# Linear attention and a token and channel mixer on one core: the first batch's intermediates are laid into buffers of later weights, and U and V are converted one pair later

## The chip, the core and the metric

The kernel runs on one core of a Trainium2 chip. The metric is the device time of one execution in microseconds (us), the median of three runs. All inputs are in DRAM at the start and the output is in DRAM at the end. A profiled execution of the kernel before is the source of the rows below.

## What is computed

```python
def phi(x):
    proj = np.einsum('bhsd,df->bhsf', x, w_phi)
    proj = proj - np.max(np.abs(proj), axis=-1, keepdims=True)
    return np.concatenate([np.exp(proj), np.exp(-proj)], axis=-1)
q_p, k_p = phi(q), phi(k)                       # q, k, v: (8, 8, 576, 64), w_phi: (64, 128)
kv = np.einsum('bhsf,bhsd->bhfd', k_p, v)
z = np.sum(k_p, axis=2)
num = np.einsum('bhsf,bhfd->bhsd', q_p, kv)
den = np.einsum('bhsf,bhf->bhs', q_p, z)[..., None] + 1e-06
x = (num / den) with heads side by side         # (8, 576, 512)
u = x + transpose(transpose(x) @ U @ V)         # U: (576, 32), V: (32, 576), mixes tokens
out = u + np.maximum(u @ w_ch1, 0.0) @ w_ch2    # (512, 2048), (2048, 512)
```

U, V, w_ch1 and w_ch2 arrive as 64-bit floats. The kernel makes 32-bit floats of their bits, and splits each into a high and a low part for matmuls of three terms.

## The kernel before, in words

**Attention.** The work goes over 8 batches of 4 pairs of heads; pair j of batch b is written `b_j` here, so 0_2 is the third pair of the first batch. For each pair a `Pair` object loads the raw k and q tiles and the rows left over by 128 (`raw`, `t_r`), transposes them on TensorE (`T`, `tail_T`), projects them (`pk`, `pq`, in PSUM), makes features (`kp` on VectorE and ScalarE; `qp` with a maximum over the partitions on GpSimd, L342), sums `kv` (L424 and L434), and writes the pair's columns of x (`xp`, L452 and L459, then L464 to L476). In every pair the chain is: raw, transposes, projections, features, kv, output. The feature of q takes: copy on ScalarE (L341), maximum on GpSimd (L342), subtraction on VectorE (L343), two exponentials on ScalarE (L344, L345).

**Token mixing.** After pair 1 and pair 3 of a batch `Tokens.split` (L524) splits half of x into high and low parts `xs` (L534, L535), `down` (L538) multiplies by U (`pp`, then `pst`), and `up` (L554) multiplies by V and adds to x.

**Channel mixing.** A `Mixer` per batch transposes x into `uT_hi`, `uT_lo` (L576) and then runs 16 times `hidden(f)` (L586, 12 matmuls into `ph`) and `add(f)` (L605, 12 matmuls into `o`). It needs the two weight tiles of block f. The chunks of one batch's mixer are laid between the attention steps of the next.

**Weights.** `weight_blocks` (L209) loads each of the 32 tiles (16 blocks f, w1 and w2) into a buffer of the tag `wide`, and converts it: ScalarE L141 and L145, VectorE L142, L147 and L150, GpSimd L155 (an add of 64-bit integers), ScalarE L227 (high part), VectorE L228 (low part). In the tables `w1_f` and `w2_f` are the tiles loaded, `w_b`, `w_r` the work tiles, `w_hi`, `w_lo` the results. The tag `wide` has four buffers (L123). They are taken in turn by the tiles of U and V (`u_st` and three `v_st`, L173 to L204), by the three `xs` tiles of each half of x (L532), and by the weights.

**What sets the order.** A scheduler of the tile framework orders the instructions of each engine from its own estimate of times. Each engine then works strictly in that order. All DMAs are issued by one queue, SyncE's (SP), in order too. A tag with n buffers makes the (n+1)th tile wait for the release of the first. From the third batch TensorE's order is written out by hand (`ordered`, L771). TensorE also runs filler matmuls on zeros (`busy`, L692).

Of the kernel before, what the change touches and what calls it, by code (L numbers as in the profile page):

```python
# [25 lines left out]
def tile_kernel(  # L26
# [212 lines left out]

    class Pair:  # L240


# [80 lines left out]
        def k_features(self, n, k_w, kp):

            ng = kp.shape[1]
# [6 lines left out]
            nc.scalar.activation(out=kp[:, :, 0:F], in_=kp[:, :, F:2 * F], func=AF.Exp)
            nc.scalar.activation(  # L333
                out=kp[:, :, F:2 * F], in_=kp[:, :, F:2 * F], func=AF.Exp, scale=-1.0)
            return kp

        def q_features(self, n, pq, m):
            nm = f"{self.nm}_{n}"
# [1 line left out]
            qp = att.tile([P, 2, m], F32, tag=tag, bufs=bufs, name=f"qp{nm}")  # L340
            nc.scalar.copy(out=qp[:, 1, :], in_=pq[:, 0:m])  # L341
            nc.gpsimd.partition_all_reduce(qp[:, 0, :], qp[:, 1, :], P, ReduceOp.absmax)  # L342
            nc.vector.tensor_sub(qp[:, 1, :], qp[:, 1, :], qp[:, 0, :])  # L343
            nc.scalar.activation(out=qp[:, 0, :], in_=qp[:, 1, :], func=AF.Exp)  # L344
            nc.scalar.activation(out=qp[:, 1, :], in_=qp[:, 1, :], func=AF.Exp, scale=-1.0)  # L345
# [557 lines left out]
```

## Time and profile before

| what | value |
|---|---|
| three runs | 1196.93, 1198.11 (median), 1198.18 us |
| profiled execution | 1194.9 us, of which the span from first to last instruction is 1193.1 us |
| busy in the span | PE 1140.7 us (96%), DVE 661.1 us (55%), ACT 529.2 us (44%), POOL 200.5 us (17%) |
| mean granted TensorE clock | 0.983 of full speed |
| from 260 us on | PE busy 923.86 of 933.10 us |

PE is TensorE, DVE VectorE, ACT ScalarE, POOL GpSimd, SPq SyncE's queue of DMA issues. In a timeline row stand start, duration, engine, line, operation, out<-in and in brackets the idle time before it with its releaser; in a windows row the busy time of each engine, its instructions, the granted clock (PEclk) and the DMA share and rate. A busy sum can be above the wall time, since consecutive instructions of an engine overlap a little.

### The profile page before, as it was taken

How to read it: one execution, taken by the hardware profiler on the slowest of the kernel's cores; microseconds unless marked ns; L12 is line 12 of the kernel's file. 1: busy time of each engine (PE TensorE's matmuls, PEld its weight loads, DVE VectorE, ACT ScalarE, POOL GpSimd, SP SyncE). 2: the span in 40 equal slices, each digit the busy share in tenths (PEclk: the TensorE clock that was granted, in tenths of full speed). 3: DMA queues.
4: the chain of work that ended last, by engine and by line, in shares of the span. 5: the costliest groups of instructions: out<-in, count | busy, mean ns of one | idle time of the engine just before them, and what ended most of it. 6: DMA issues, size and time to landing. Idle time of an engine off the chain costs nothing.

```text
span 1193.1 us, 22535 instructions
## 1 busy us (share of the span) xinstructions
PE 1140.7 (96%) x9308; PEld 947.4 (79%) x9316; DVE 661.1 (55%) x1339; ACT 529.2 (44%) x1134; POOL 200.5 (17%) x151
## 2 busy tenths in 40 slices
PE   7966998989999999999999999999999999999997
PEld 5635776768888888888888888888888888888886
DVE  6669789755655665565557555656655644112111
ACT  5767586634543454445453445355434532111110
POOL 2434254301111111102210112011111110000000
PEclk9988999999999999999999999999999999999999
DMA  4345153421112211221122111311121003100001
GB/s 119 88 147 183 48 181 92 140 72 31 31 57 66 81 31 31 90 70 32 33 65 96 34 37 49 104 40 32 54 91 49 28 2 124 39 1 25 11 1 36
DMA packets 90534, 75.75 MB, mean 63 GB/s; under 512 B 51648, under 2 KB 76736, under 8 KB 90304
## 3 DMA queue, kind: packets, MB, share of 16 engines
q1 hardware_dynamic: 90432, 74.31, 20.4%
q8 instruction: 74, 1.21, 0.4%
q14 instruction: 28, 0.23, 0.1%
HBM read 55.41 MB, written 18.87 MB: 62 GB/s over the span
## 4 chain that ended last, share of the span: by engine, by line
PE 83%; DVE 9%; DMA 3%; ACT 2%; issue 1%; SPq 1%; POOL 0%; POOLq 0%; DVEq 0%; ACTq 0%
PE ph L593 31%; PE o L612 31%; PE xp L459 4%; PE kv_ps L434 4%; DMA w<-in_moe_w_ch_dram 2%; PE T L308 2%; PE pk L391 2%; DVE w_r L150 1%; PE pp L548 1%; DVE w_lo L228 1%; DVE w_b L142 1%; PE pt L580 1%; PE kv_ps L424 1%; DVE w_r L147 1%; PE pq L415 1%
## 5 line engine op out<-in xcount | busy, mean ns | idle before, releaser
L593 PE MATMUL ph<-uT_hi,w_hi 128*128 128x512 f32 x576 | 230.6, 400 | 10.5 <-ACT uT_hi L234 5.3
L612 PE MATMUL o<-w_hi,h_hi 128*128 128x512 f32 x576 | 233.0, 405 | 4.1 <-ACT h_hi L599 4.1
L600 DVE SCALAR_TENSOR_TENSOR h_lo<-ph,h_hi 128x512 fp32r<-128x512 f32 x144 | 99.2, 689 | 244.0 <-ACT h_hi L599 243.9
L593 PE MATMUL ph<-uT_lo,w_hi 128*128 128x512 f32 x576 | 226.0, 392 | 0.9 <-DVE uT_lo L235 0.9
L612 PE MATMUL o<-w_lo,h_hi 128*128 128x512 f32 x576 | 226.9, 394 | 0.0
L593 PE MATMUL ph<-uT_hi,w_lo 128*128 128x512 f32 x576 | 226.3, 393 | 0.0
L612 PE MATMUL o<-w_hi,h_lo 128*128 128x512 f32 x576 | 220.5, 392 | 0.0
L599 ACT ACTIVATE h_hi<-ph 128x512 fp32r<-128x512 f32 x144 | 86.0, 597 | 272.9 <-PE ph L593 272.6
L593 PEld LDWEIGHTS ph<-uT_hi,w_hi 128*128 128x128 f32 x576 | 109.0, 189 | 34.7 <-DVE h_lo L600 7.3
L342 POOL PARTITION_ALL_REDUCE qp<-qp x64 | 128.5, 2019 | 46.7 <-ACT qp L341 45.0
L612 PEld LDWEIGHTS o<-w_hi,h_hi 128*128 128x128 f32 x576 | 109.0, 189 | 28.9 <-ACT h_hi L599 6.2
L342 POOL PARTITION_ALL_REDUCE qp_t<-qp_t x32 | 24.8, 774 | 619.4 <-ACT qp_t L341 619.4
L593 PEld LDWEIGHTS ph<-uT_hi,w_lo 128*128 128x128 f32 x576 | 108.8, 189 | 24.4 <-issue 0.8
L593 PEld LDWEIGHTS ph<-uT_lo,w_hi 128*128 128x128 f32 x576 | 109.0, 189 | 22.3 <-DVE uT_lo L235 1.2
L612 PEld LDWEIGHTS o<-w_hi,h_lo 128*128 128x128 f32 x576 | 107.6, 188 | 23.4 <-DVE h_lo L600 0.3
L612 PEld LDWEIGHTS o<-w_lo,h_hi 128*128 128x128 f32 x576 | 109.4, 190 | 20.6 <-issue 0.8
L277 DVE TENSOR_TENSOR T<-T,T 64x512 fp32r<-64x512 f32 x96 | 66.2, 689 | 29.9 <-ACT T L276 27.2
L459 PE MATMUL xp<-kv,qp 128*64 128x65 f32 x2048 | 70.6, 228 | 6.7 <-DVE kp L329 2.4
L459 PEld LDWEIGHTS xp<-kv,qp 128*64 128x64 f32 x2048 | 66.7, 144 | 9.4 <-issue 3.7
L276 ACT CAST T<-T 64x512 fp32r<-64x512 f32 x96 | 55.9, 582 | 36.8 <-PE T L308 20.4
L434 PEld LDWEIGHTS kv_ps<-vb,kp 128*64 128x64 f32 x2048 | 64.4, 138 | 2.4 <-ACT kp L333 0.8
L434 PE MATMUL kv_ps<-vb,kp 128*64 128x65 f32 x2048 | 66.1, 222 | 0.0
(127 smaller groups left out, 1493.8 us busy)
## 6 DMA issues: line engine op xcount, KB each, us to landing
w<-in_moe_w_ch_dram SPq DMA_DIRECT2D x32, 512.0 KB, 3.9
raw<-in_k_dram SPq DMA_DIRECT2D x32, 256.0 KB, 2.9
raw<-in_q_dram SPq DMA_DIRECT2D x32, 256.0 KB, 2.7
vb<-in_v_dram SPq DMA_DIRECT2D x64, 128.0 KB, 3.0
u_dram<-x SPq DMA_DIRECT2D x32, 256.0 KB, 2.6
st<-u_dram SPq DMA_DIRECT2D x16, 512.0 KB, 4.0
out_dram<-st SPq DMA_DIRECT2D x32, 256.0 KB, 2.5
t_r<-in_k_dram SPq DMA_DIRECT2D x32, 32.0 KB, 2.1
```

Of the source, the lines that this page charges most:

```text
L142: nc.vector.tensor_scalar(out=bh[:, :, 1], in0=halves[:, :, 3], scalar1=0x7FF0, scalar2=None, op0=ALU.bitwise_and)
L276: nc.scalar.copy(out=dst[0:D], in_=src)
L277: nc.vector.tensor_sub(dst[D:2 * D], src, f32(dst[0:D]))
L308: nc.tensor.transpose(out=pT[:, c * P:(c + 1) * P], in_=self.raw[n][:, c // 2, c % 2, :], identity=ident)
L342: nc.gpsimd.partition_all_reduce(qp[:, 0, :], qp[:, 1, :], P, ReduceOp.absmax)
L391: nc.tensor.matmul(pk[:, i, :, :], self.T[0][:, i, cs], w_hl, start=True, stop=True)
L434: nc.tensor.matmul(self.kv_v[z * HP:(z + 1) * HP, f, g, :], kp[:, i, f * F + z * HP:f * F + (z + 1) * HP], self.vb[:, g, t, :], start=Fals ...
L459: nc.tensor.matmul(xv[zs, c, :], qp[:, f, c * P + z * HP:c * P + (z + 1) * HP], self.kv[:, f, c // 2, :], start=(f == 0), stop=(f == 1), s ...
L593: nc.tensor.matmul(ph, l[:, c * P:(c + 1) * P], r[:, c, :], start=(n == 0), stop=(n == len(terms) * NCC - 1))
L599: nc.scalar.activation(out=h_hi, in_=ph, func=AF.Relu)
L600: nc.vector.scalar_tensor_tensor(out=h_lo, in0=ph, scalar=0.0, in1=f32(h_hi), op0=ALU.max, op1=ALU.subtract)
L612: nc.tensor.matmul(self.o[t], l[:, cs], r, start=(f == 0 and n == 0), stop=(f == NFC - 1 and n == len(terms) - 1))
```

## The change

Tiles of batch 0 (`raw`, `t_r`, `tail_T`, `T`, features `kp` and `qp`, and `xs`) no longer come from the pools `raw`, `att` and `wide`. They lie in tiles of the pool `const` whose tags belong to the weights of blocks 15 down to 5 (`KEEP = 5`; for block f these are `wh1_f`, `wh2_f` and the `wl` tiles). A weight tile of block 5 or later can be converted into such a place once the first batch's tile there is released. Raw tiles have a place per pair, the transposes and features a place per parity of the pair, the `xs` tiles one place each (five, instead of three shared buffers). Features of batch 0 are kept as two tiles of half the width each. `load_uv()` stands after the first `narrow` (output of pair 0_0 and kv of pair 0_1) instead of ahead of pair 0_0's kv.

```diff
+    KEEP = 5
+    homes = [f"wh{m}_{f}" for f in range(NFC - 1, KEEP - 1, -1) for m in (1, 2)]
+    homes += [f"wl{i}" for i in range(2 * NFC, 2 * KEEP, -1)]
+    home_of = {}
+
+    def home(key, shape, name, dt=F32):
+
+        if key not in home_of:
+            home_of[key] = homes.pop(0)
...
+        t = const.tile([P, C], dt, tag=home_of[key], name=name)[:, 0:n]
...
+                if b == 0:
+                    m = home(("raw", j, n), (2, NT // 2, 2 * D), f"raw{nm}_{n}")
...
+            if self.b == 0:
+                self.tail_T = home(("tail_T", self.par), (2, P), f"tail_T{nm}")
...
+            if self.b == 0 and ng > 1:
+                return [
+                    home(("kp", self.par, n, i), (ng, F), f"kp{self.nm}_{n}{i}") for i in range(2)]
...
-                if t % 2 == 0:
-                    xs2 = wide(f"xs{b}_{i}_{t}", (2, 2, C // 2), F32R)
-                xs = xs2[:, t % 2]
+                if b == 0:
+                    xs = home(("xs", t), (2, C // 2), f"xs{b}_{i}_{t}", F32R)
+                else:
+                    if t % 2 == 0:
+                        xs2 = wide(f"xs{b}_{i}_{t}", (2, 2, C // 2), F32R)
+                    xs = xs2[:, t % 2]
...
         nxt.transpose_k()
-        load_uv()
         cur.s_kv()
...
             step(narrow, nxt, cur, x, xt)
+            if n == 0:
+                load_uv()
```

The scheduler lays out the first two batches anew. The instructions are the same in number and kind; up to the fourth hidden block of batch 0's mixer (`ph0_3`) TensorE's order differs, from there on it is the same in both kernels. In the rows below a name ends in a buffer number; a feature of the changed kernel has one digit more for its half (`qp0_2_01` is the second half of pair 0_2's first q feature).

VectorE between the output of pair 0_1 and the q feature of pair 0_2, before:

```order
L464 TENSOR_SCALAR den0_1_1_614<-xp1_0_1_597 128x4
L465 RECIPROCAL den0_1_1_614<-den0_1_1_614 128x4
L470 TENSOR_TENSOR x0_335<-xp1_0_1_597,den0_1_1_614 128x2x2x64
L535 TENSOR_TENSOR xs0_0_0_661<-x0_335,xs0_0_0_661 128x256
L535 TENSOR_TENSOR xs0_0_2_666<-x0_335,xs0_0_2_666 128x256
L535 TENSOR_TENSOR xs0_0_4_671<-xt0_336,xs0_0_4_671 128x256
L535 TENSOR_TENSOR xs0_0_0_661<-x0_335,xs0_0_0_661 128x256
L535 TENSOR_TENSOR xs0_0_2_666<-x0_335,xs0_0_2_666 128x256
L441 COPY kv0_2_655<-kv_ps0_2_618 128x260
L343 TENSOR_TENSOR qp0_2_0_686<-qp0_2_0_686 128x512
```

The last rows of that stretch on VectorE in the changed kernel:

```order
L228 TENSOR_TENSOR w_lo1_2_1417<-w_r1_2_1409,w_hi1_2_1416 128x512
L150 SCALAR_TENSOR_TENSOR w_r2_4_1553<-w2_4_1550,w_r2_4_1553 128x512
L150 SCALAR_TENSOR_TENSOR w_r1_5_1656<-w1_5_1653,w_r1_5_1656 128x512
L584 TENSOR_TENSOR xs0_0_1_677<-x0_279,xs0_0_1_677 128x256
L228 TENSOR_TENSOR w_lo2_2_1431<-w_r2_2_1423,w_hi2_2_1430 128x512
L584 TENSOR_TENSOR xs0_0_3_683<-x0_279,xs0_0_3_683 128x256
L142 TENSOR_SCALAR w_b1_6_1802<-w1_6_1800 128x512
L228 TENSOR_TENSOR w_lo1_3_1462<-w_r1_3_1454,w_hi1_3_1461 128x512
L228 TENSOR_TENSOR w_lo2_3_1476<-w_r2_3_1468,w_hi2_3_1475 128x512
L228 TENSOR_TENSOR w_lo1_4_1547<-w_r1_4_1539,w_hi1_4_1546 128x512
L228 TENSOR_TENSOR w_lo2_4_1561<-w_r2_4_1553,w_hi2_4_1560 128x512
L389 TENSOR_TENSOR qp0_2_01_702<-qp0_2_01_702,qp0_2_00_701 128x512
```

Between the k features of pair 0_2 and the subtraction of its first q feature (L343 before, L389 after) no weight stood on VectorE; now all four VectorE steps of the ten tiles of blocks 0 to 4 stand there, and three steps of blocks 5 and 6. Before, the first weight step on VectorE came after the `xs` of the batch's second half, and 14 tiles lay between there and the third hidden block.

ScalarE around the copy of pair 0_2's q projection, before:

```order
L333 ACTIVATE kp0_2_1_559<-kp0_2_1_559 128x4x128
L534 CAST xs0_0_0_661<-x0_335 128x256
L534 CAST xs0_0_2_666<-x0_335 128x256
L534 CAST xs0_0_4_671<-xt0_336 128x256
L345 ACTIVATE qp0_2_t_676<-qp0_2_t_676 128x128
L341 COPY qp0_2_0_686<-pq0_0_2_682 128x512
```

And in the changed kernel:

```order
L141 ACTIVATE w_b2_4_1552<-w2_4_1550 128x512
L227 CAST w_hi1_3_1461<-w_r1_3_1454 128x512
L583 CAST xs0_0_1_677<-x0_279 128x256
L583 CAST xs0_0_3_683<-x0_279 128x256
L227 CAST w_hi2_3_1475<-w_r2_3_1468 128x512
L145 ACTIVATE w_b2_4_1552<-w_b2_4_1552,warm_75 128x512
L227 CAST w_hi1_4_1546<-w_r1_4_1539 128x512
L387 COPY qp0_2_01_702<-pq0_0_2_697 128x512
```

The copy that the maximum on GpSimd waits for now stands behind the steps of nine tiles and two steps of the tenth.

SyncE's queue where the first weights are loaded, before:

```order
L258 DMA t_r1_1_930<-in_q_dram 64x2x64
L271 DMA vt1_91<-in_v_dram 64x64 x2
L268 DMA vb1_92<-in_v_dram 128x4x64 x2
L217 DMA w1_0_1326<-in_moe_w_ch1_dram 128x4x256
L221 DMA w2_0_1340<-in_moe_w_ch2_dram 128x1024
L271 DMA vt0_85<-in_v_dram 64x64 x2
```

And in the changed kernel:

```order
L284 DMA t_r1_0_762<-in_q_dram 64x2x64
L217 DMA w1_0_1350<-in_moe_w_ch1_dram 128x4x256
L221 DMA w2_0_1364<-in_moe_w_ch2_dram 128x1024
L217 DMA w1_1_1378<-in_moe_w_ch1_dram 128x4x256
L221 DMA w2_1_1392<-in_moe_w_ch2_dram 128x1024
L217 DMA w1_2_1406<-in_moe_w_ch1_dram 128x4x256
L221 DMA w2_2_1420<-in_moe_w_ch2_dram 128x1024
```

The first weights now stand ahead of the loads of pair 1_1 and right behind those of pair 1_0.

More of the change, by code (lines that the diff above doesn't have):

```diff
@@ L249, in __init__ @@
             for n, src in enumerate((k, q)):
-                m = raw.tile([P, 2, NT // 2, 2 * D], F32, tag="raw", bufs=2, name=f"raw{nm}_{n}")
+                if b == 0:
+                    m = home(("raw", j, n), (2, NT // 2, 2 * D), f"raw{nm}_{n}")
+                else:
+                    m = raw.tile(
+                        [P, 2, NT // 2, 2 * D], F32, tag="raw", bufs=2, name=f"raw{nm}_{n}")
                 nc.sync.dma_start(
@@ L254, in __init__ @@
                 self.raw.append(m)
-            self.t_r = raw.tile([P, 2 * D], F32, tag="t_r", bufs=1, name=f"t_r{nm}")
+            if b == 0:
+                self.t_r = home(("t_r", j), (2 * D,), f"t_r{nm}")
+            else:
+                self.t_r = raw.tile([P, 2 * D], F32, tag="t_r", bufs=1, name=f"t_r{nm}")
             for n, src in enumerate((k, q)):
@@ L289, in transpose_k @@
                 self.T = [self.transpose(0)]
+            elif self.b == 0:
+                self.T = [
+                    self.transpose(n, home(("T", self.par, n), (SM,), f"T{n}_{nm}"))
+                    for n in range(2)]
             else:
@@ L319, in k_tile @@
         def k_tile(self, n, ng):
+            if self.b == 0 and ng > 1:
+                return [
+                    home(("kp", self.par, n, i), (ng, F), f"kp{self.nm}_{n}{i}") for i in range(2)]
+            if self.b == 0:
+                kp = home(("kp", self.par, n), (2, 1, F), f"kp{self.nm}_{n}")
+                return [kp[:, i] for i in range(2)]
             tag, bufs = ("feat", 4) if ng > 1 else ("feat_t", 2)
-            return att.tile([P, ng, 2 * F], F32, tag=tag, bufs=bufs, name=f"kp{self.nm}_{n}")
+            kp = att.tile([P, ng, 2 * F], F32, tag=tag, bufs=bufs, name=f"kp{self.nm}_{n}")
+            return [kp[:, :, i * F:(i + 1) * F] for i in range(2)]
         def k_features(self, n, k_w, kp):
-            ng = kp.shape[1]
+            ng = kp[0].shape[1]
             mk = small.tile([P, 16], F32, tag="mk", name=f"mk{self.nm}_{n}")[:, 0:ng]
@@ L339, in q_features @@
             tag, bufs = ("feat", 4) if m == SM else ("feat_t", 2)
[L340 to L345, printed above, removed]
+            if self.b == 0 and m == SM:
+                qp = [home(("qp", self.par, n, i), (m,), f"qp{nm}{i}") for i in range(2)]
+            elif self.b == 0:
+                qp = home(("qp", self.par, n), (2, m), f"qp{nm}")
+                qp = [qp[:, i, :] for i in range(2)]
+            else:
+                qp = att.tile([P, 2, m], F32, tag=tag, bufs=bufs, name=f"qp{nm}")
+                qp = [qp[:, i, :] for i in range(2)]
+            nc.scalar.copy(out=qp[1], in_=pq[:, 0:m])
+            nc.gpsimd.partition_all_reduce(qp[0], qp[1], P, ReduceOp.absmax)
+            nc.vector.tensor_sub(qp[1], qp[1], qp[0])
+            nc.scalar.activation(out=qp[0], in_=qp[1], func=AF.Exp)
+            nc.scalar.activation(out=qp[1], in_=qp[1], func=AF.Exp, scale=-1.0)
             return qp
@@ L385, in project_k @@
             kp = self.k_tile(g, NT)
-            k_w = kp[:, :, F:2 * F]
+            k_w = kp[1]
             for s in range(2):
@@ L393, in project_k @@
                 ts_ = slice(2 * s, 2 * s + 2)
-                nc.scalar.copy(out=kp[:, ts_, 0:F], in_=pk[:, :, 1, :])
+                nc.scalar.copy(out=kp[0][:, ts_, :], in_=pk[:, :, 1, :])
                 nc.vector.tensor_tensor(
-                    out=k_w[:, ts_, :], in0=pk[:, :, 0, :], in1=kp[:, ts_, 0:F], op=ALU.add)
+                    out=k_w[:, ts_, :], in0=pk[:, :, 0, :], in1=kp[0][:, ts_, :], op=ALU.add)
             return self.k_features(g, k_w, kp)
```

30 lines of the change are left out of this document (20 added, 10 removed).

## The prediction

> **What bounds the kernel now.** I read the page's first part, then the busy time by stretches, with cuts where an instruction named below begins or ends.
>
> ```profile
> span 1193.1 us, 22535 instructions
> 15.50:36.00 20.50, 14.82 (x259) 11.82 (x257) 16.60 (x55) 12.02 (x31) 5.04 (x5) 0.92 0.42 115
> 36.00:44.30 8.30, 7.60 (x141) 5.40 (x142) 7.49 (x20) 7.04 (x18) 2.95 (x3) 1.00 0.03 8
> 44.30:69.40 25.10, 21.67 (x373) 16.86 (x375) 18.12 (x44) 18.60 (x42) 8.30 (x6) 1.00 0.37 103
> 69.40:97.00 27.60, 14.55 (x57) 8.30 (x56) 19.95 (x35) 18.32 (x35) 10.91 (x8) 0.78 0.67 216
> 97.00:106.90 9.90, 9.86 (x68) 8.10 (x68) 9.90 (x17) 7.28 (x13) 5.47 (x3) 0.58 0.48 164
> 106.90:137.30 30.40, 23.54 (x186) 17.81 (x185) 25.28 (x40) 18.75 (x35) 12.94 (x10) 0.94 0.26 77
> 260.00:1193.10 933.10, 923.86 (x7282) 780.74 (x7282) 458.72 (x938) 361.11 (x796) 107.62 (x69) 1.00 0.16 47
> ```
>
> The columns are PE, PEld, DVE, ACT, POOL, then clock, DMA share and GB/s. From 260 us on TensorE is busy 923.86 of 933.10 us: nothing is to be had there, and what an early stretch wins or loses reaches the end whole. The change acts ahead of 137.3 us, where the fourth hidden block (`ph0_3`) starts and the two orders become one. There TensorE stands idle for 13.05 us in 69.4 to 97.0 and for 6.9 us in 106.9 to 137.3, and in the 9.9 us between it runs at a clock of 0.58.
>
> Next, the chain of waits from 60 to 110 us, and SyncE's issues:
>
> ```profile
> by line: DMA w<-in_moe_w_ch_dram 29.6%; DVE w_r L150 10.4%; DVE w_b L142 10.4%; DVE w_r L147 9.8%; DVE w_lo L228 5.2%; issue 5.1%; DVE x L565 5.0%; DVE uT_lo L235 3.9%; DVE mk L327 3.9%; ACT kp L332 3.6%; ACT kp L333 3.3%; DVE kp L329 2.4%;
> 58.41 0.56 SPq L217 DMA_DIRECT2D w<-in_moe_w_ch_dram  x1
> 67.32 0.35 SPq L221 DMA_DIRECT2D w<-in_moe_w_ch_dram  x1
> 72.39 0.37 SPq L217 DMA_DIRECT2D w<-in_moe_w_ch_dram  x1
> 77.84 0.35 SPq L221 DMA_DIRECT2D w<-in_moe_w_ch_dram  x1
> 83.96 0.37 SPq L217 DMA_DIRECT2D w<-in_moe_w_ch_dram  x1
> ```
>
> Weights are 29.6% of these 50 us as transfers (14.8 us) and 35.8% as conversion on VectorE (17.9 us). The second to fifth tiles are issued one by one, 5 to 6 us apart, each as the tile ahead of it is converted: the `xs` tiles hold the three other buffers of `wide`. So the stall before is a string of load, convert, load, convert, with the mixer's start behind it.
>
> **The change part by part.** The sum compares the time at which `ph0_3` starts; it is made against the profiled execution (1194.9 us, 3.2 below the median of 1198.11).
>
> *A. U and V one pair later.* These rows show kv of pair 0_0 done on TensorE and its copy on VectorE:
>
> ```profile
> 16.10 1.97 PE L434 MATMUL kv_ps<-vb,kp 128*64 128x65 f32 x60
> 22.36 0.42 DVE L441 COPY kv<-kv_ps 128x260 f32<-128x260 f32 x1
> 37.23 1.28 DVE L329 TENSOR_TENSOR kp<-pk,mk 128x512 f32<-128x512 f32 x2
> ```
>
> The sums end at 18.07 and the copy comes at 22.36, behind steps of U and V. By the new order two k features, the second q feature and two steps of U come ahead of the copy; I put it at 19.4. But the conversion of U and V is only moved, not removed: it now delays the q projection's copy on ScalarE and pair 0_1's subtraction. Of 3 us I keep 2.6 at the end of pair 0_2's k features (38.5 before, 35.9 now). Were all lost it is 0; were V's DMAs late, 2 us the other way. V's twelve issues also stand ahead of pair 0_3's raw tiles on SyncE; these are used 20 us later, so that costs nothing.
>
> *B. Ten tiles ahead of pair 0_2's q feature.* `xs` no longer holds `wide`, so the four buffers are free as U and V are done. Weights load from about 32 us (the queue reaches them behind pair 1_0's loads), four in flight. But VectorE then has all four steps of ten tiles between pair 0_2's k features and the subtraction of its q feature. What ten tiles cost when they come densely is shown by the groups from 87.8 to 128 us, beside the shortest, median and longest of one step:
>
> ```profile
> L228 DVE TENSOR_TENSOR w_lo<-w_r,w_hi 128x512 fp32r<-128x512 f32 x11 | 11.7, 1060 | 0.2
> L147 DVE TENSOR_SCALAR w_r<-w 128x512 int32<-128x512 int32 x10 | 7.3, 732 | 0.0
> L150 DVE SCALAR_TENSOR_TENSOR w_r<-w,w_r 128x512 int32<-128x512 int32 x10 | 6.8, 678 | 0.0
> L142 DVE TENSOR_SCALAR w_b<-w 128x512 uint16<-128x512 uint16 x10 | 6.6, 660 | 0.7 <-DMA w<-in_moe_w_ch_dram 0.6
> L147 DVE TENSOR_SCALAR w_r<-w x32: 402/410/1522, 66.1 to 235.3; 128x512 int32<-128x512 int32 x32
> L228 DVE TENSOR_TENSOR w_lo<-w_r,w_hi x32: 661/692/1731, 69.4 to 243.8; 128x512 fp32r<-128x512 f32 x32
> L155 POOL INT64_ADD w_r<-w_r,w_b x32: 1262/1299/2762, 67.4 to 238.3; - x32
> 44.30 1.42 DVE L343 TENSOR_TENSOR qp<-qp 128x512 f32<-128x512 f32 x1
> 68.58 0.76 DVE L535 TENSOR_TENSOR xs<-x,xs 128x256 fp32r<-128x256 f32 x2 [0.47 <-ACT xs L534]
> ```
>
> A tile takes 1.06 + 0.73 + 0.68 + 0.66 = 3.13 us, ten 31.3. Three more weight steps (2.1) and the attention steps that stood there before (VectorE's 7.49 us from 36.0 to 44.3, less 2.5 for the k features, 5.0) make 38.4 us of busy time. VectorE's 19 groups of that dense stretch, of which these are the four largest, add up to 45.5 us in 40.2 of wall, a ratio of 1.13, so this takes 34 us: from 35.9 to 69.9. Before, the same subtraction began at 44.30. Loss: 25.6 us, A included.
>
> About 0.9 us of each 3.13 is a step made longer: its medians are 0.41, 0.69, 0.68 and 0.46, together 2.24, and single steps reach 1.5 and 1.7 us beside GpSimd's work. The Trainium skill's page "SBUF — State Buffer", section "Who interferes with whom", says that a two-port VectorE step and a GpSimd step lock each other out for a whole instruction, and so does a VectorE step with two SBUF inputs beside a GpSimd read; the spread from 402 to 1522 ns agrees. By that rule, with an add of 1.3 us per tile, ten tiles would cost up to 22.4 + 13 = 35.4 us in place of 31.3, and the sum 3.6 us more. I keep the measured mean. Without collisions B is 8 us shorter (10 x 0.9 by 1.13).
>
> *C. From there to the end of the second half's `xs`.* Before: 44.30 to 69.34, 25 us. The same attention chain stands there now, without the first tile's three VectorE steps at 65.8 (about 1.5 us), but with ScalarE steps of blocks 5 and 6 between pair 0_3's features. I take 25 again; 2 us either way. `xs` ends at 95.
>
> *D. From `xs` to the end of the first hidden block.* Before: 69.34 to 106.9, 37.5 us, with the string of loads in it. Its TensorE work is 14.55 us at a clock of 0.78 and 9.86 at 0.58, so 11.3 + 5.7 = 17 at full clock.
>
> ```profile
> 83.31 2.14 PE L548 MATMUL pp<-xs,u_all 128*128 128x256 f32 x10
> 97.04 0.80 PE L593 MATMUL ph<-uT_hi,w_hi 128*128 128x512 f32 x1 [4.57 <-ACT uT_hi L234]
> 106.57 0.39 PE L593 MATMUL ph<-uT_hi,w_lo 128*128 128x512 f32 x1
> ```
>
> With four tiles left, half converted, VectorE and ScalarE hold the path little: I take 17.2 us, and the block ends at about 112.2. Gain 20.3. The floor is the 17; if four tiles' remains and the transposes' copies queue, 23.
>
> *E. From there to `ph0_3`.* Before 30.4 us, with 6.9 idle and some at half clock (0.94 in the mean). Now nothing of blocks 1 to 3 is left to convert, so I take TensorE's 23.5 less 0.6 for the clock: 22.9, `ph0_3` at 135.1. Gain 7.5; if the feature of pair 1_1 makes it wait as it did before, 3.
>
> Sum: +25.6 + 0 - 20.3 - 7.5 = -2.2 us. The profiled execution would take 1192.7, the median 1198.11 - 2.2 = 1195.9.
>
> **The rivals.** A measurement of this kernel can tell about 0.2%, 2.4 us, from no change.
>
> *1. The weights hide (faster).* Speaks for it: VectorE is idle for 3.9 + 0.8 + 7.0 + 7.65 = 19.3 us between 15.5 and 97 us, and a scheduler laid the new steps there. If GpSimd's adds collide less while the q chain waits, B is 8 us shorter and the result 10.2 us faster, 1187.9. Against: the one dense stretch before, in which a tile cost 3.13 us and not 2.24.
>
> *2. TensorE goes cold while it waits for pair 0_2 (slower).* Before, it is busy 21.67 of 25.10 us in the middle stretch at a clock of 1.00. Now it has nothing but a kv sum and a projection from about 48 to 64 us. What a pause of 4.5 us does is shown here:
>
> ```profile
> 69.93 1.12 PE L378 MATMUL pq<-T,w_f 64*128 64x512 f32 x2
> 75.52 2.07 PE L378 MATMUL pq<-T,w_f 64*128 64x512 f32 x2 [4.47 <-DVE kv L441]
> ```
>
> The same two matmuls took 1.12 and then 2.07 us. Of the 21.67 us in which TensorE is busy in the middle stretch I estimate 8.5 to lie on the path; the rest is filler or stands beside features. If the clock stays at half through C, they take 17 and 8.5 us are added; less 2.2 that is 6.3 us slower, 1204.4. It can be told from no change from 4.6 us added on, half clock over half of that path. Against: the filler matmuls kept 1.00 there before. The Trainium skill's page "TensorE: Matmul & The Clock Gate", section "What's actually happening", says that an idle window of about 3.4 us halves the clock until about 3.4 us of busy time have passed; the rows above agree. By that rule a pause costs at most 1.7 us once work is dense, and three pauses about 5, so the forecast would become 1200.9, on this rival's side.
>
> *3. It doesn't do what it says: no change.* If conversions and attention only change places on VectorE, and pauses there are as long as before (within 2.4 us), the time stays. For it: the same steps are done by the same engines, and A to E cancel to 2.2 us, with 25.6 on one side and 27.8 on the other.
>
> **How the numbers follow.** Forecast with its bounds, half of it beyond 2.4 us (1190.5 to 1199.5): 0.48. Rival 1: 0.18. Rival 2: 0.24. Rival 3: 0.10. Faster by over 0.2%: 0.18 + 0.24 = 0.42. Within: 0.10 + 0.20 = 0.30. Slower: 0.24 + 0.04 = 0.28. The range takes in rival 1 and most of rival 2: 1187 to 1203.5.
>
> **What would show it.** Right: weight loads from about 32 us, several in flight; the copy of kv 0_0 at about 19.4; pair 0_2's q subtraction at 65 to 72; no idle time on weights' DMAs; `ph0_0` ending at 109 to 115 and `ph0_3` starting at 131 to 138; from there the same distance to the end, 1055.8 us. Wrong: the subtraction before 60 (rival 1); a clock under 0.8 from 65 to 95 with `ph0_3` after 140 (rival 2); a distance from `ph0_3` to the end that differs by over 2 us, since then the change acts where I have none.

## The result, and the profile after

The changed kernel takes 1207.22 us (median of 4 runs, 1204.81 to 1208.24); the kernel before, beside it, 1197.52 (4 runs, 1195.54 to 1198.18). The ratio is 1.0081, with a 95% interval of 1.006 to 1.0102: 9.7 us slower, where 2.2 us faster was forecast. Two executions in this document took far longer than the rest (1426 us of the kernel before, 3953 us of e2, the profiled one) and are left out of all times. The profiled execution took 1204.81 us with a span of 1202.7 (before 1194.9 and 1193.1).

The steps of the prediction, each by the event that ends it (us; in brackets how long the step took):

| step, and what ends it | before | forecast | after |
|---|---|---|---|
| A: pair 0_2's k features end | 38.5 | 35.9 | 38.8 |
| B: its q subtraction starts | 44.3 (5.8) | 69.9 (34.0) | 75.7 (36.8) |
| C: second half's `xs` ends | 69.3 (25.0) | 95 (25) | 103.6 (27.9) |
| D: first hidden block `ph0_0` ends | 107.0 (37.6) | 112.2 (17.2) | 126.8 (23.2) |
| E: `ph0_3` starts | 137.3 (30.4) | 135.1 (22.9) | 147.3 (20.5) |
| rest of the span | 1055.8 | 1055.8 | 1055.4 |

So the whole difference lies ahead of `ph0_3`, as forecast. The busy time by stretches, with cuts at these events (columns as in the prediction: length, then PE, PEld, DVE, ACT, POOL, clock, DMA share, GB/s):

```profile
15.50:38.80 23.30, 16.43 (x284) 12.85 (x282) 19.25 (x58) 14.14 (x35) 5.92 (x6) 0.91 0.54 146
38.80:75.70 36.90, 17.91 (x165) 13.56 (x165) 36.27 (x61) 28.19 (x52) 18.24 (x12) 0.60 0.57 187
75.70:103.60 27.90, 22.00 (x327) 16.82 (x325) 17.75 (x45) 19.14 (x41) 6.06 (x4) 0.88 0.13 34
103.60:126.80 23.20, 18.20 (x148) 12.63 (x146) 18.28 (x32) 11.41 (x26) 9.29 (x7) 0.93 0.31 90
126.80:147.30 20.50, 20.50 (x186) 16.23 (x186) 7.01 (x16) 9.05 (x20) 4.90 (x4) 1.00 0.23 62
260.00:1202.70 942.70, 932.30 (x7331) 787.92 (x7329) 465.70 (x951) 364.86 (x804) 107.78 (x69) 1.00 0.16 48
```

Read the second row first: in B VectorE is busy for 36.27 of 36.90 us, and TensorE for half of it at a clock of 0.60. So the attention waits for VectorE here. The chain of waits from 60 to 110 us no longer holds a weight transfer (29.6% before):

```profile
by line: PE kv_ps L480 9.2%; PE xp L505 9.2%; DVE w_lo L228 9.2%; issue 9.1%; DVE w_r L147 5.8%; ACT w_b L145 5.0%; DVE qp L389 4.7%; PE pq L424 4.3%; ACT T L349 4.2%; PE busy L741 4.1%; DVE w_r L150 4.0%; POOL qp L388 3.9%; DVE w_b L142 3.
```

SyncE's issues show why: the loads start at 34.9 us, four within 1.7 us, where before they came one by one from 58.41 on:

```profile
34.92 0.53 SPq L217 DMA_DIRECT2D w<-in_moe_w_ch_dram  x1
35.56 0.44 SPq L221 DMA_DIRECT2D w<-in_moe_w_ch_dram  x1
36.10 0.37 SPq L217 DMA_DIRECT2D w<-in_moe_w_ch_dram  x1
36.58 0.45 SPq L221 DMA_DIRECT2D w<-in_moe_w_ch_dram  x1
41.20 0.37 SPq L217 DMA_DIRECT2D w<-in_moe_w_ch_dram  x1
```

And VectorE's groups in B (38.8 to 75.7 us) show what it does there:

```profile
L228 DVE TENSOR_TENSOR w_lo<-w_r,w_hi 128x512 fp32r<-128x512 f32 x10 | 10.0, 995 | 0.3
L150 DVE SCALAR_TENSOR_TENSOR w_r<-w,w_r 128x512 int32<-128x512 int32 x11 | 8.4, 775 | 0.0
L142 DVE TENSOR_SCALAR w_b<-w 128x512 uint16<-128x512 uint16 x11 | 8.4, 760 | 0.3 <-DMA w<-in_moe_w_ch_dram 0.2
L147 DVE TENSOR_SCALAR w_r<-w 128x512 int32<-128x512 int32 x11 | 7.4, 674 | 0.0
```

A tile's four steps take 0.995 + 0.775 + 0.760 + 0.674 = 3.20 us (3.13 forecast). These rows add up to 34.2 us; with the attention's steps VectorE's groups add up to 40.7 us in 36.8 of wall, since consecutive steps overlap.

Two more places matter. At the front, pair 0_1's q projection does run earlier on TensorE (27.64 us, 29.52 before), but V's conversion now stands between it and all that follows, on ScalarE (L145) and on VectorE (L157 and those around it):

```profile
27.64 1.13 PE L424 MATMUL pq<-T,w_f 64*128 64x512 f32 x4
29.72 0.37 ACT L145 ACTIVATE v_st<-v_st,warm 128x64 uint16<-128x64 uint16 x1 [0.76 <-DVE v_st L142]
29.97 1.05 ACT L387 COPY qp<-pq 128x512 f32<-128x512 f32 x2
32.64 1.18 DVE L157 CUSTOM_DVE_ANT_0 v_st<-v_st 128x128 uint16<-128x128 uint16 x1
35.77 0.68 DVE L389 TENSOR_TENSOR qp<-qp,qp 128x512 f32<-128x512 f32 x1
```

The first q subtraction of pair 0_1 comes at 35.77 us, where it came at 33.33 before: TensorE's gain of 1.9 us is gone. And in D, steps of the weights whose places `xs` holds wait on VectorE for pp0_1 (idle time and releaser in the bracket). Five of them run ahead of the `pst` step that the path needs:

```profile
109.17 2.17 DVE L147 TENSOR_SCALAR w_r<-w 128x512 int32<-128x512 int32 x3 [2.77 <-PE pp L597]
111.26 1.28 DVE L150 SCALAR_TENSOR_TENSOR w_r<-w,w_r 128x512 int32<-128x512 int32 x2
112.57 0.42 DVE L601 TENSOR_TENSOR pst<-pp,pst 32x256 fp32r<-32x256 f32 x1
```

### The profile page after: what moved, and what is told of

Read it like the earlier page. It is cut to its first block, busy times and chain, and to the rows that moved or that the text cites. A ratio compares the mean times of both kernels' runs of the same rounds, so it can differ in the third digit from the quotient of the medians.

```text
span 1202.7 us, 22531 instructions
## 1 busy us (share of the span) xinstructions
PE 1141.4 (95%) x9316; PEld 949.2 (79%) x9316; DVE 663.1 (55%) x1339; ACT 528.8 (44%) x1134; POOL 199.5 (17%) x151
## 3 DMA queue, kind: packets, MB, share of 16 engines
q1 hardware_dynamic: 90432, 74.31, 20.3%
## 4 chain that ended last, share of the span: by engine, by line
PE 84%; DVE 9%; ACT 2%; SPq 2%; DMA 2%; issue 1%; POOL 0%; DVEq 0%; POOLq 0%
PE ph L642 31%; PE o L661 31%; PE xp L505 5%; PE kv_ps L480 4%; PE pk L437 2%; PE T L341 2%; DVE w_r L150 2%; DVE w_lo L228 1%; DMA w<-in_moe_w_ch_dram 1%; PE pp L597 1%; DVE w_r L147 1%; DVE w_b L142 1%; PE kv_ps L470 1%; PE pt L629 1%; PE pq L461 1%
## 5 line engine op out<-in xcount | busy, mean ns | idle before, releaser
L661 PEld LDWEIGHTS o<-w_lo,h_hi 128*128 128x128 f32 x576 | 108.4, 188 | 20.3 <-issue 0.8
L505 PE MATMUL xp<-kv,qp 128*64 128x65 f32 x2048 | 73.2, 232 | 12.1 <-ACT qp L390 8.5
L303 DVE TENSOR_TENSOR T<-T,T 64x512 fp32r<-64x512 f32 x96 | 66.2, 689 | 29.9 <-ACT T L302 27.2
```

What stands on the lines that cost most here:

```text
L303: nc.vector.tensor_sub(dst[D:2 * D], src, f32(dst[0:D]))
L505: nc.tensor.matmul(xv[zs, c, :], qp[f][:, c * P + z * HP:c * P + (z + 1) * HP], self.kv[:, f, c // 2, :], start=(f == 0), stop=(f == 1), s ...
L661: nc.tensor.matmul(self.o[t], l[:, cs], r, start=(f == 0 and n == 0), stop=(f == NFC - 1 and n == len(terms) - 1))
```

## The experiments

The change has three parts: U and V one pair later ("U" below), two pairs at once in the weights' places ("P"), and `xs` in such places instead of `wide` ("X"). Ratios are against runs of the kernel before on the same chip; 1% is 12 us. "Steps ahead" are VectorE's weight steps (56 for blocks 0 to 6) that stand in its queue ahead of the end of batch 0's second `xs`; in the kernel before they are three, the first tile's from 65.75 us on, not none as the section on the change has it. "Front" is the time from the span's start to that end, "back" the time from there to `ph0_3`. Each edit makes the scheduler lay out the first two batches anew, so that a run can differ in more than the part it is named for.

**e1, without X.**

```
-                if b == 0:
-                    xs = home(("xs", t), (2, C // 2), f"xs{b}_{i}_{t}", F32R)
-                else:
...
+                if t % 2 == 0:
+                    xs2 = wide(f"xs{b}_{i}_{t}", (2, 2, C // 2), F32R)
+                xs = xs2[:, t % 2]
```

> The changed kernel, but the xs tiles of batch 0 lie in the buffers of wide again, as before the change; all other tiles of batch 0 keep their new places, and U and V stay one pair later. So the weights wait for xs again: no weight step is queued on VectorE ahead of the q subtractions of pairs 0_2 and 0_3 (43 and 47 in the changed kernel). Theory 1, the early conversion costs more than it brings: the loss goes, 1195 to 1199 us, pair 0_2's subtraction near 45 us and the stall behind xs as before (ph0_3 at 136 to 139). Theory 2, U and V one pair later, or the tiles' new places, cost it: at least 1203 us with ph0_3 past 143.

Measured: 1195.74 us, ratio 0.9989 (0.9979 to 0.9998). The loss is gone, as theory 1 said. But the front is not that of before: the q subtraction comes at 52.13 us, not near 45, because TensorE takes the projection behind the kv sum of pair 0_2, and that sum behind pair 0_1's outputs, which come late (before, the projection was at 39.57 us):

```profile
44.69 3.16 PE L480 MATMUL kv_ps<-vb,kp 128*64 128x65 f32 x64
48.32 1.13 PE L424 MATMUL pq<-T,w_f 64*128 64x512 f32 x4
52.13 1.66 DVE L389 TENSOR_TENSOR qp<-qp,qp 128x512 f32<-128x512 f32 x1 [0.67 <-POOL qp L388]
```

`xs` ends at 78.0 us (69.3 before), and `ph0_3` starts at 137.0: U and P together lengthen the front by 8.7 us with no more weight steps there than before (3), and the back gives 9.0 back.

**e2, without U.**

```
+        load_uv()
         cur.s_kv()
...
             step(narrow, nxt, cur, x, xt)
-            if n == 0:
-                load_uv()
```

> The changed kernel, but U and V are loaded and converted where they were before the change, ahead of pair 0_0's kv sum; everything else as changed. The weights then start earlier as well: 19 weight steps stand on VectorE ahead of pair 0_2's k features, and still 43 ahead of its q subtraction. Theory 1, U and V are only moved and the early weights are the loss: 1205 to 1209 us, no change against the changed kernel beyond 2.4 us. Rival, the later U and V cost some 3 us in front (the raw tiles' k features end at 38.8 and not at 35.9) and hold the weights back: 1202 to 1204.5 us, the q subtraction of pair 0_2 near 72 in place of 75.7.

Measured: 1210.74 us, ratio 1.0112 (1.0095 to 1.013): 3.7 us slower than the changed kernel's 1.0081, above what either side expected. Its stages are not known. The two intervals overlap, so that no more follows than this: beside P and X the earlier U and V are no gain, and the rival falls.

**e3, `xs` in the places of the last blocks.**

```
-    home_of = {}
+    home_of = {("xs", t): homes.pop(0) for t in range(NT + 1)}
```

> The changed kernel, but the five xs tiles of batch 0 lie where the weights of the last blocks come (15, 14 and the first of 13) and not where those of blocks 5 to 7 come; the other tiles move up the list by five. The weights of blocks 5 and 6 then need not wait for pp0_1 and stand ahead of xs on VectorE (47 steps ahead of pair 0_2's q subtraction in place of 43, all 56 ahead of the end of xs). Theory, the three waiting steps ahead of pst cost stage D about 3 us: pst follows pp0_1 within 0.6 us, D takes 19.5 to 20.5 in place of 23.2, and B 2 to 3 more for the four steps; 1204 to 1208 us. Rival, D is long for another reason (GpSimd and ScalarE beside the transposes): D stays above 22 us and the whole is 1208 to 1211 us.

Measured: 1201.93 us, ratio 1.0045 (1.0032 to 1.0058), faster than either side expected. Here D and the whole back, and the `pst` step, in the stretches and the timeline:

```profile
107.37:123.42 16.05, 14.88 (x87) 10.50 (x90) 10.69 (x21) 9.98 (x22) 4.89 (x4) 1.00 0.43 129
107.37:146.59 39.22, 38.05 (x318) 28.79 (x319) 17.62 (x39) 19.30 (x42) 9.91 (x8) 1.00 0.31 90
...
113.06 0.42 DVE L601 TENSOR_TENSOR pst<-pp,pst 32x256 fp32r<-32x256 f32 x1 [3.46 <-ACT pst L600]
```

`pst` waits for ScalarE's copy alone, and D takes 16.05 us in place of 23.2. No weight step is left in D, where nine stood in the changed kernel: five ahead of `pst` and four behind it. Those ahead account for the 3 us expected (`pst` comes 5.7 us after `xs` ends, 8.9 in the changed kernel); the other 4 us come behind `pst`. B is 4.3 us longer for the added steps (38.31 to 79.42) and E 2.7, so `ph0_3` comes only 0.7 us earlier (146.59); the rest of the span is 2.1 us shorter, for which no step was found. In the back TensorE is now busy for 38.05 of 39.22 us at a clock of 1.00: there is little more to win there.

**e4, more filler matmuls.**

```
-                keep_busy(2, True)
+                keep_busy(8, True)
```

> The changed kernel with eight filler matmuls instead of two behind each step of batch 0, so that TensorE pauses less and its clock is less often halved. Theory 1, VectorE sets stage B (36.3 of 36.9 us busy) and the clock only stretches TensorE's own part of stages C and D: the granted clock in stage B rises from 0.60 to 0.8 or more, and the time falls by no more than 3 us, 1204 to 1208 us. Rival, the cold clock is the loss (the prediction's second rival): with the clock up the time falls by 5 us or more, to 1202 us or less.

Measured: 1211.0 us, ratio 1.0121 (1.0103 to 1.0139). The stretches of B (from 47.99 us, where pair 0_2's k features now end) and C:

```profile
47.99:73.93 25.94, 15.24 (x133) 10.26 (x135) 25.86 (x46) 19.19 (x37) 15.31 (x10) 0.70 0.58 171
73.93:106.11 32.18, 31.25 (x402) 20.74 (x406) 20.93 (x51) 22.53 (x47) 7.75 (x5) 1.00 0.13 33
```

C has its full clock and takes 32.2 us in place of 27.9, since the fillers themselves fill TensorE (31.25 us busy). The scheduler's order changed too: eight weight steps now stand ahead of the k features, where none did. So this run can't price the clock. It shows that VectorE is B's limit at another clock too (25.86 of 25.94 us). Neither side expected the whole to be slower.

**e5 to e7, fewer steps ahead.** The places of `xs` decide which blocks wait for it; k is 0, 1 and 3:

```
-    home_of = {}
+    home_of = {("xs", t): f"wh{t % 2 + 1}_{k + t // 2}" for t in range(NT + 1)}
```

> The changed kernel with the xs tiles of batch 0 in the places of blocks 0 to 2, whose first VectorE result must wait until pp0_1 has read xs. So four weight tiles load early and wait in the buffers of wide, and only 8 weight steps (two for each) stand on VectorE ahead of pair 0_2's q subtraction, 43 in the changed kernel; 14 ahead of pst, 35 ahead of the last transpose's step. Theory, each step queued ahead of the attention delays it by about 0.85 us (36.9 us for 43), and the string of loads is gone anyway: the subtraction starts near 51, xs ends near 79, the first hidden block ends near 106, ph0_3 starts at 133 to 137 and the whole takes 1193 to 1197 us. Rival, it is the loads in flight and not the steps that slow the front, or conversion behind xs costs D all that it saves: ph0_3 past 140, 1200 us or more.

> As the run before, with xs in the places of blocks 1 to 3: the two tiles of block 0 are converted early, 16 weight steps ahead of pair 0_2's q subtraction. Theory: the subtraction near 58, xs ends near 85, D is shorter (22 to 25 us), ph0_3 at 134 to 139, 1194 to 1199 us; time rises with the number of early steps once VectorE has no idle time left ahead of the subtraction. Rival, early steps are free as long as they fill idle time (about 7 us before 45 us): no later than the run with 8 steps in the q subtraction by over 3 us, and 3 us faster or more in the whole.

> As the runs before, with xs in the places of blocks 3 to 5: 32 weight steps ahead of pair 0_2's q subtraction. Theory: the subtraction near 68, xs ends near 96, D 19 to 22, ph0_3 at 138 to 143, 1199 to 1204 us, on a line between the run with 8 steps and the changed kernel. Rival, the loss comes from the last blocks only (their places are xs's, the three steps ahead of pst): 1196 us or less.

Measured: 1194.05, 1195.82 and 1202.69 us, ratios 0.9978 (0.9967 to 0.9989), 1.0 (0.999 to 1.001) and 1.0057 (1.0044 to 1.0071); q subtractions at 52.44, 55.20 and 66.54 us, `xs` ends at 75.3, 79.5 and 90.3, `ph0_3` at 133.9, 137.5 and 142.9. The more steps ahead, the slower, on a line to the changed kernel, as theory had it. D is not as expected (34.3, 37.3 and 37.0 us): the held blocks' steps now stand ahead of the transposes' steps. e5 lies 2.6 us under the kernel before and 12.3 under the changed one (0.0022 and 0.0103 of 1196). e1 above and e10 below lie under the kernel before too, and the three intervals overlap: nothing shows that X held back like this is better than no X. Stage C of e5 is 22.85 us long, at the full clock:

```profile
52.44:75.29 22.85, 21.32 (x356) 16.29 (x357) 15.79 (x40) 15.55 (x36) 6.49 (x4) 1.00 0.17 43
```

**e8, X alone** (the kernel before, with `home` and the lines that e1 takes out; `xs` in the places of blocks 15, 14 and 13).

> The kernel before the change, and of the change only the xs tiles of batch 0 in the places of the last blocks' weights (15, 14 and the first of 13): the buffers of wide are free early, all else stands as before (raw tiles, transposes and features in their old buffers, U and V early). 38 weight steps then stand on VectorE ahead of pair 0_2's k features (none in the changed kernel) and all 56 ahead of the end of xs. Theory, the early conversion is the loss: it is slower than before too, 1200 to 1208 us. Rival, the loss needs the two pairs at once or the later U and V: 1198 us or less.

Measured: 1205.26 us, ratio 1.0077 (1.0064 to 1.009). X alone makes almost the whole loss, with neither of the other parts, as theory had it. `xs` ends at 109.5 us and `ph0_3` starts at 148.2, 10.9 later than before.

**e9, U alone, and e10, P alone.** e9 is the kernel before with `load_uv()` moved as in the change; e10 is e1 with `load_uv()` at its old place as in e2.

> The kernel before the change, and of the change only U and V one pair later. Theory from the run with xs in wide (there pair 0_1's first q subtraction came 1.9 us later than before, the second 3.7, and pair 0_2's 7.8): the later U and V themselves do this, since V's steps now stand ahead of pair 0_1's q copy on ScalarE and ahead of its subtraction on VectorE. Pair 0_2's k features end at 38 to 38.6 (no gain), its q subtraction starts at 50 to 53 in place of 44.3. The whole 1195 to 1199 us, since the weights' first tiles find free stretches behind. Rival, the prediction's step A: the k features end near 36 and the subtraction near 42, 1193 to 1196 us.

> The changed kernel with xs in wide and U and V at their old place, so that of the change only the places of the raw tiles, transposes and features are left, two pairs at once. Theory: without the later U and V the q subtraction of pair 0_2 is back near 44 to 45 and xs ends near 70; two pairs at once bring nothing by themselves, 1195 to 1198 us, within 2.4 us of before. Rival, two pairs at once are what delays the q subtraction (TensorE takes its projection behind the kv sum): 50 to 53 again.

Measured: e9 1202.56 us, ratio 1.0051 (1.0038 to 1.0065); e10 1194.14, ratio 0.9985 (0.9976 to 0.9994). In e9 the k features end at 45.1 us (38 to 38.6 expected), the q subtraction comes at 51.70, `xs` ends at 77.1. Here is V's conversion on VectorE, with pair 0_1's kv copy behind it and TensorE waiting for that copy:

```profile
33.88 1.15 DVE L204 TENSOR_TENSOR v_all<-v_st,v_all 32x64 fp32r<-32x64 f32 x1
35.06 0.43 DVE L441 COPY kv<-kv_ps 128x260 f32<-128x260 f32 x1
35.55 1.12 PE L308 MATMUL T<-ident,raw 128*128 128x128 f32 x4 [3.28 <-DVE kv L441]
```

The kv sums were done at 29.5 us (27.39 + 2.11). So the later U and V lengthen the front by 7.7 us by themselves; the prediction's step A is refuted in sign. `ph0_3` is still 2 us earlier than before (135.3); the loss of e9, which neither side expected, comes after it (1066.1 us to the end in place of 1055.8). It arises ahead of 302 us: up to there from `ph0_3` TensorE is busy for 147.15 of 166.68 us, in the same stretch of the kernel before for 144.29 of 156.65. Which order on VectorE causes it is not known. In e10 the q subtraction is at 46.60, `xs` ends at 73.0 and `ph0_3` starts at 134.0, between theory (44 to 45, `xs` near 70) and its rival (50 to 53); the whole is a little faster than theory had it (1195 to 1198).

**e11, e5 with U and V early** (e5's line, `load_uv()` as in e2).

> The run with 8 early steps (xs in the places of blocks 0 to 2), but with U and V at their old place. Theory: the front gets back the 8 us that the later U and V cost pair 0_2's q feature (subtraction near 47, after the 8 steps; xs ends near 70), D and E stay as they are with U and V late (34 and 24 us), so ph0_3 near 128 to 131 and the whole 1188 to 1193 us. Rival, what the front wins VectorE's weight steps take again (the same steps in less time): ph0_3 at 132 to 136, 1193 to 1197 us.

Measured: 1202.13 us, ratio 1.0055 (1.0043 to 1.0068), against theory: pair 0_2's k features end at 48.7 and its q subtraction comes at 57.85. VectorE stands for 8.76 us at the first of the early weight steps, whose load has not landed; e15 below shows the same.

**e12, blocks from 1 on held until the transposes** (on e3):

```
+    for i in range(4):
+        g = const.tile([P, C], F32, tag=f"wh{i % 2 + 1}_{1 + i // 2}", name=f"gate{i}")[:, 0:P]
+        nc.scalar.copy(out=g, in_=ident)
+        gates.append(g)
...
-                    identity=ident)
+                    identity=gates[c] if self.g == 0 else ident)
```

> The changed kernel with xs in the places of the last blocks, and four copies of the identity in the places of blocks 1 and 2, which the transposes of batch 0's mixer read: blocks from 1 on can't be finished ahead of these transposes. 16 weight steps stand ahead of pair 0_2's q subtraction and of the end of xs, 20 ahead of the last transpose's step (54 in the changed kernel), 43 ahead of the first hidden block's h_lo (56). Theory, a stage's length goes with the steps queued ahead of its last item on VectorE, about 0.75 us each: xs ends near 80, D takes 17 to 20 us, ph0_0 ends near 98, E is longer (28 to 36), ph0_3 at 128 to 134, 1187 to 1194 us. Rival, VectorE's work up to ph0_3 sets its time whatever the order: ph0_3 at 136 to 140, 1195 to 1200 us.

Measured: 1195.75 us, ratio 0.9996 (0.9987 to 1.0005). D and E in the stretches:

```profile
79.79:97.61 17.82, 15.87 (x126) 11.62 (x127) 13.21 (x26) 14.82 (x29) 8.62 (x7) 1.00 0.65 205
97.61:133.76 36.15, 24.81 (x177) 19.13 (x178) 33.90 (x53) 26.25 (x49) 19.58 (x14) 0.76 0.31 96
```

D is short as soon as hardly a weight step stands ahead of the transposes' last step (17.8 us, with four short ones there), and E then has VectorE as its limit (33.90 of 36.15 us). The stages came out as theory expected, `ph0_3` too (133.8), but from there the rest takes 1059.8 us in place of 1055.8: the whole is no faster, and lies in the rival's range.

**e13, U and X** (e9 with X as in e8).

> The kernel before the change with U and V one pair later and the xs tiles of batch 0 in the places of the last blocks, without two pairs at once. 30 weight steps stand ahead of pair 0_2's k features, all 56 ahead of the end of xs. Theory, what moving xs costs (9 us alone, 11 beside the two other parts) stands whatever else is changed: 1204 to 1214 us. Rival, the later U and V hold the weights back so far that moving xs costs little: under 1202 us.

Measured: 1205.22 us, ratio 1.0079 (1.0066 to 1.0092), within theory's range; but X adds only 3.3 us to U (1.0079 less 1.0051). Up to `ph0_3` it adds 13.7 (149.0, 135.3 in e9); the 10 us that e9 loses behind `ph0_3` are not there in e13 (1054.0 us to the end).

**e14 and e15, hardly a step ahead, loads in flight:**

```
-    home_of = {}
+    home_of = {("xs", t): n for t, n in enumerate(("wl1", "wl2", "wl3", "wl4", "wh1_0"))}
```

> The changed kernel with xs in the places that the first steps of the first tiles write (both the w_r places of blocks 0 and 1 and one w_b place), so that only 3 short weight steps stand on VectorE ahead of pair 0_2's q subtraction and of the end of xs, while four tiles lie loaded in the buffers of wide. Theory, the steps and not the loads are the cost: the q subtraction near 51 to 52, xs ends near 76 to 78, behind it nothing waits for a load, ph0_3 at 132 to 136, 1192 to 1196 us. Rival, the early loads cost something themselves: ph0_3 past 138, over 1198 us.

> As the run before, with U and V at their old place. Theory: the front is that of two pairs at once alone (q subtraction at 46 to 48, xs ends near 73), and the loads in flight shorten what follows: ph0_3 at 130 to 134, 1188 to 1194 us. Rival: as in the run with 8 early steps and U and V early, VectorE stands in its queue at a weight step whose load comes late, pair 0_2's k features end past 45, and the whole takes over 1198 us.

Measured: e14 1200.08 us, ratio 1.0034 (1.0022 to 1.0047); e15 1200.06, ratio 1.0033 (1.002 to 1.0046). Both go to the rivals. In e15 VectorE stands at the head of its queue at weight steps whose loads are not there yet (idle time and releaser in brackets), with pair 0_1's q subtraction and pair 0_2's k features behind them:

```profile
39.52 0.46 DVE L142 TENSOR_SCALAR w_b<-w 128x512 uint16<-128x512 uint16 x1 [9.21 <-DMA w<-in_moe_w_ch_dram]
41.11 0.46 DVE L142 TENSOR_SCALAR w_b<-w 128x512 uint16<-128x512 uint16 x1 [1.13 <-DMA w<-in_moe_w_ch_dram]
42.89 0.89 DVE L142 TENSOR_SCALAR w_b<-w 128x512 uint16<-128x512 uint16 x1 [1.32 <-DMA w<-in_moe_w_ch_dram]
43.67 0.67 DVE L389 TENSOR_TENSOR qp<-qp,qp 128x512 f32<-128x512 f32 x1
```

At these three short steps VectorE waits for 11.7 us. The Trainium skill's page "PSUM — Partial Sum Buffer", section "Engine vs sequencer instructions", says that VectorE's queue is strictly first in, first out; these rows agree, and so do the steps ahead of `pst` in the changed kernel. In e14 the front is that of e1 (`xs` ends at 78.8 us), but the back takes 64.1 us against 59.0 there, with the same steps left to do. They stand in another order: 29 of them run in D against 21 in e1, and D is 34.8 us long against 27.1. Why the back as a whole is longer is not settled.

## Why the prediction was wrong

All versions in one table (us). Front, back, `ph0_3` and rest are of one profiled execution each, which lies up to 2.8 us off its version's median (e10 and e14), so they and the ratio don't add up exactly. "X at 0", "at 1" and "at 3" are the k of e5 to e7, "X last" is the places of e3, "X at `w_r`" those of e14:

| run | parts | steps ahead | front | back | `ph0_3` | rest | ratio |
|---|---|---|---|---|---|---|---|
| before | none | 3 | 69.3 | 68.0 | 137.3 | 1055.8 | 1 |
| e10 | P | 4 | 73.0 | 61.0 | 134.0 | 1055.4 | 0.9985 |
| e9 | U | 3 | 77.1 | 58.3 | 135.3 | 1066.1 | 1.0051 |
| e1 | U P | 3 | 78.0 | 59.0 | 137.0 | 1057.3 | 0.9989 |
| e14 | U P, X at `w_r` | 3 | 78.8 | 64.1 | 142.9 | 1058.0 | 1.0034 |
| e15 | P, X at `w_r` | 3 | 82.5 | 61.8 | 144.3 | 1055.8 | 1.0033 |
| e5 | U P, X at 0 | 8 | 75.3 | 58.6 | 133.9 | 1060.3 | 0.9978 |
| e11 | P, X at 0 | 8 | 82.6 | 58.6 | 141.2 | 1059.0 | 1.0055 |
| e6 | U P, X at 1 | 16 | 79.5 | 58.1 | 137.5 | 1055.1 | 1.0 |
| e12 | U P X, held | 16 | 79.8 | 54.0 | 133.8 | 1059.8 | 0.9996 |
| e7 | U P, X at 3 | 32 | 90.3 | 52.6 | 142.9 | 1057.4 | 1.0057 |
| after | U P X | 47 | 103.6 | 43.7 | 147.3 | 1055.4 | 1.0081 |
| e4 | U P X, filler | 47 | 106.1 | 49.5 | 155.6 | 1054.7 | 1.0121 |
| e2 | P X | not known | | | | | 1.0112 |
| e3 | U P, X last | 56 | 107.4 | 39.2 | 146.6 | 1053.3 | 1.0045 |
| e8 | X | 56 | 109.5 | 38.7 | 148.2 | 1054.0 | 1.0077 |
| e13 | U X | 56 | 110.3 | 38.7 | 149.0 | 1054.0 | 1.0079 |

The plan of the sum was right: a long front against a short back, and nothing behind `ph0_3`. It forecast +25.7 us for the front and -27.9 for the back, and +34.3 and -24.3 came. The miss of 12.2 us at `ph0_3` is 2.9 in A, 2.8 in B, 2.9 in C and 6.0 in D, less 2.4 in E.

**Step A failed in sign.** The prediction put the later U and V at a gain of 2.6 us, with 2 us of loss as the worst. The copy of kv 0_0 did come early (20.60 us, 22.36 before), but the k features end at 38.8 us, no earlier than before (38.5). In the front, U costs 7.7 us alone (e9), 5.0 beside P (e1 against e10) and 0.8 beside X (e13 against e8); it gains in none of them, and what it costs depends on what stands beside it. V's steps moved to a place where pair 0_1's kv copy, q copy and q subtraction stand behind them. I took credit for what TensorE does earlier and left out what the moved steps stand ahead of.

**Steps B and C were near, but 5.7 us short together.** Of B's 2.8 us a part is in the sum: VectorE's groups there add up to 40.7 us where 38.4 were put, 34.2 for the weights in place of 33.4 and 6.5 for the attention in place of 5.0. The attention's 5.0 was busy time, in which overlaps count once already, and it was divided by the overlap again. For C's 2.9 us the clock would account in size: TensorE's 22.00 us there at 0.88 would be 2.6 us shorter at full clock, an estimate from that row. It is not shown. At a clock of 1.00, C took anything from 22.85 (e5) to 26.43 us (e10), e4 left aside; in e14 it took 24.75 at 0.86, with less of TensorE's work.

**Step D failed in size: 23.2 us for 17.2, and E gives 2.4 back.** The prediction saw that four tiles would be left, put VectorE's part at next to nothing and named 23 as the worse case; the worse case came. Nine weight steps run in D. The first wait for `xs` at the head of VectorE's queue, ahead of `pst`, and the others stand between the steps of the transposes. In e3 none is left, D takes 16.05 us, and the back is 39.2 us, 28.8 less than before, where 27.9 were forecast. So without the nine steps the back comes out near its forecast, 4.4 us shorter than in the changed kernel; D alone is 7 us shorter, with fewer of TensorE's matmuls in it (87 for 148). This is shown; the waiting, the work and the order of these steps are not told apart.

**X is the loss.** U and P together leave `ph0_3` where it was (137.0 us in e1, 137.3 before). X moves it by 10.9 us alone (e8), by 10.3 beside U and P (from e1 to the changed kernel) and by 13.7 beside U (from e9 to e13). In the front X costs 40.2, 25.6 and 33.2 us in these three settings, and the back gives 29.3, 15.3 and 19.6 of it back.

**Why the two sides don't cancel.** From e6 to e3 40 more steps stand ahead; the front grows by 27.9 us, 0.70 per step, and the back shrinks by 18.9, 0.47 per step. The back of before and after, each as one stretch, shows why:

```profile
69.34:137.35 68.01, 48.05 (x310) 34.21 (x309) 55.13 (x91) 44.39 (x82) 29.32 (x21) 0.82 0.46 146
...
103.62:147.28 43.66, 38.66 (x331) 28.82 (x325) 25.27 (x47) 20.46 (x45) 14.19 (x11) 0.96 0.27 77
```

The change takes 55.13 - 25.27 = 29.9 us of VectorE's work out of the back and wins 24.3 us, since part of that work lay beside TensorE's own. X moves 29.0 us of it (54.23 in e1's back, 25.27 after); in the front, where TensorE waits for VectorE, this work costs 25.6 us, and U and P have spent 9 us of what the back can give. With U and P in place, X can win at most about 59.0 - 38.7 = 20.3 us there (TensorE's own work in the row above), and did win 15.3. That decides the sign.

**The rivals.** The first (weights hide, 1187.9 us) is refuted: VectorE is busy for 36.27 of 36.90 us in B. The third (no change) by the interval. The second (TensorE cold, 1204.4) came nearest in time, and its sign came too: a clock under 0.8 from 65 to 95 us with `ph0_3` after 140.

```profile
65.00:95.00 30.00, 23.44 (x233) 17.26 (x233) 22.07 (x43) 20.65 (x44) 11.01 (x8) 0.77 0.23 67
65.00:75.70 10.70, 7.32 (x36) 6.03 (x38) 10.39 (x14) 5.65 (x12) 6.82 (x4) 0.51 0.32 102
75.70:95.00 19.30, 16.12 (x203) 11.22 (x199) 11.68 (x31) 15.00 (x32) 4.18 (x4) 0.91 0.18 48
```

But the cold part lies in B, where VectorE is busy for 10.39 of 10.70 us and TensorE waits for it. In C, which this rival expected at half clock with 8.5 us added, the clock is 0.88, and the cost is 2.6 us by the estimate above. So the mechanism was not this one. From the Trainium skill's page "TensorE: Matmul & The Clock Gate", section "What's actually happening", the prediction worked out at most 1.7 us for a pause; by that estimate the 2.6 us would be one and a half pauses, which no run here shows.

**What stays open.** What lengthens C by 2.9 us, why U costs 7.7 us in one setting and 0.8 in another, e14 against e1 (5 us in the back with the same steps left), e9's 10 us behind `ph0_3`, and the several us by which the rest differs among e5, e12 and before.

## What to carry to other kernels

Work that an in-order engine takes earlier lengthens the stretch in front wherever another engine waits for it (25.6 us here, for 29.0 of work moved), and shortens the stretch behind only as far as the other engine stood idle there (15.3 us). Before you move it, work out TensorE's own floor of the later stretch (38.7 us here against 68.0), since no more than the difference can come back, and count what other parts of the change have already taken of it. When a step is moved, list what stands behind it in each queue at the new place, a step that waits for a load or for a buffer above all: VectorE waited 11.7 us at three short steps in e15, and nine weight steps left in D cost the back 4.4 us (e3). A buffer that looks like a bottleneck may be what keeps such work in its place: widening it was the loss here, and holding the work by another dependency (e5) took the loss away.

## What the runs showed of the hardware that was not expected

The same small VectorE step took about five times as long in two places beside GpSimd's reduce. L157 on 128x128 and L204 on 32x64 took 0.22 us each before the change, when GpSimd was idle:

```profile
26.33 0.22 DVE L157 CUSTOM_DVE_ANT_0 v_st<-v_st 128x128 uint16<-128x128 uint16 x1
27.94 0.22 DVE L204 TENSOR_TENSOR v_all<-v_st,v_all 32x64 fp32r<-32x64 f32 x1
```

In the changed kernel L157 took 1.18 us (at 32.64, above), and in e9 L204 took 1.15 (at 33.88, above), each while GpSimd ran its reduces; here those of the changed kernel, and its own L204 on 32x64:

```profile
30.63 3.88 POOL L388 PARTITION_ALL_REDUCE qp<-qp  x2 [13.54 <-ACT qp L387]
34.41 0.82 POOL L388 PARTITION_ALL_REDUCE qp_t<-qp_t  x1
34.98 0.22 DVE L204 TENSOR_TENSOR v_all<-v_st,v_all 32x64 fp32r<-32x64 f32 x1
```

That the reduce is the reason is argued from the times alone, and the last two rows speak against a simple rule: beside the shorter reduce the step took its 0.22 us. The Trainium skill's page "SBUF — State Buffer", section "Who interferes with whom", says that a VectorE step with two SBUF inputs contends with a GpSimd instruction that reads SBUF; L204 is such a step; its row in e9 agrees, its row in the changed kernel does not.
